# GFNet mixing and SoLU block: the step back in even and odd halves on quarters of the array, and the second product in another PSUM bank

## The chip, the cores and the metric

The kernel runs on one core of a Trainium2 chip. The metric is the device time in microseconds (us). Six names of engines are used: PE is TensorE's matmul stream, PEld its weight loads (they overlap the matmuls), DVE is VectorE, ACT ScalarE, POOL GpSimd, and SP the engine that only issues DMAs. Each engine takes its own instructions in order; across engines they are held together by semaphores.

## What is computed

The first half filters eight sequences of 3136 tokens with 256 channels by a multiplication in frequency space; the second is a feed-forward block over all 25088 tokens with the SoLU activation and a layer norm.

```python
X = np.fft.rfft(x, axis=1)                      # x: (8, 3136, 256)
y = np.fft.irfft(X * (filt_r + 1j * filt_i), n=3136, axis=1)
h = y.reshape(25088, 256) @ w_in                # w_in: (256, 1024)
e = np.exp(h - h.max(-1)); sm = e / (e.sum(-1) + 1e-9)
solu = h * sm
ln = (solu - solu.mean(-1)) / np.sqrt(solu.var(-1) + 1e-6) * g_ln
out = ln @ w_out                                # w_out: (1024, 256)
```

All of it is in float32.

## The kernel before

**The transform.** 3136 = 49 x 64. An example is transformed in three steps: a first one over the 49 residues (`first` or `first_quarters`), the spectrum (`forward`, `multiply`, `inverse`, seven units an example), and the step back over 49 (`fetch_back`, then `back`). Between the steps the rows lie in DRAM (`d1`, `d2`). The step back of an example has 8 pieces of 4 columns. A piece reads 100 rows (25 frequencies of four kinds) with all 256 channels. For each half of the channels (`cb`), `back` makes one matmul for each of the 4 columns: the rows are the stationary operand (100 x 128), and the table `wi_t` (100 x 98) streams. The 98 results are 49 tokens of column n and 49 tokens of the mirrored column 63 - n; the table holds both signs. ACT copies the 128 x 392 result into `y`, the SBUF buffer that holds two examples, channels on partitions.

**The block.** Tokens are taken 128 at a time; one such tile is a step k, and there are 196 steps and 9 more to empty the pipeline. Two steps, an even one k = 2j and the odd one behind it, make a pair j. For a pair, both products (with w_in and with w_out) are made by Strassen's scheme with seven multiplications each: `product(j, m)` and `project(p, m)`, m = 1 to 7. They are issued in the order 1, 5, 2, 6, 3, 4, 7 (even step: products 1, 2, 6, 7 and projections 5, 3, 4; odd step: products 5, 3, 4 and projections 1, 2, 6, 7). `keep` and `keep_out` copy an unfinished sum out of its PSUM bank on ACT, `finish` and `finish_out` take the last one on DVE and add what was kept. A bank goes on accumulating after it was read: products 1, 6, 5, 3 share bank 0, product 2 has bank 1, products 7 and 4 share bank 2; projections have two banks. So a later product must wait until the reader of the sum before has read its bank. Of one tile DVE makes: `finish` (L701 or L704) with the running minimum, `normalize` (L723, L725, L728), `turn` (L738, a transpose in blocks of 32). ACT makes the exponential (L712) and the square sum (L730). SP regroups the turned rows by DMA, POOL forms the sums that Strassen's scheme needs (L658).

**The order.** It is written out by hand in `step(k)`. The transform of examples 1 to 7 is spread over the steps by PLAN; its parts are put into lists by step: `stores` (ahead of the step's first product), `products` (in the middle), `early` (behind it, ahead of the next products), `late` and `loads` (at the end). In an even step with a step back, `back` of the first half of the channels stands in `early` and that of the second half in `late`; `forward` stands in `early` too, `multiply(i, 0)` in `late`, and `multiply(i, 1)`, `inverse`, `difference` and `first_quarters` in the odd step behind. Example 1 has its step back at steps 16 to 22, odd ones too.

**PSUM.** Eight banks: two of tag `t` (products 2, the step back, the first transform), two for a unit of the spectrum, two in `ps_m` (banks 0 and 2 of the products), two for the projections.

**Lines.** L353 step-back matmul, L356 its copy; L680 products, L792 projections; L690 `keep`, L804 `keep_out`; L701 and L704 `finish`; L809 `finish_out` with nothing kept, L811 with a kept part; L313 to L315 `multiply`; L245 `difference`; L260 `first_quarters` and L265 its copies; L292 `forward` (`pb`) and `inverse` (`pc`).

Of the kernel before, what the change touches and what calls it, by code (L numbers as in the profile page):

```python
# [9 lines left out]
FP32 = mybir.dt.float32  # L10
I32 = mybir.dt.int32
AFT = mybir.ActivationFunctionType
ALU = mybir.AluOpType
# [4 lines left out]
P = 128  # L18
B, S, C = 8, 3136, 256
# [30 lines left out]
def dft_tables():  # L50

    n1, s, q, m = np.arange(N1), np.arange(NS), np.arange(NQ), np.arange(NH)
    ph = 2 * np.pi * (np.outer(n1, s) % N1) / N1
    w = np.cos(ph), -np.sin(ph)
    v = 2 * np.cos(ph), -2 * np.sin(ph)
    v[0][:, 0], v[1][:, 0] = 1.0, 0.0
    wf = np.zeros((2, N1, NS, 4))
    wi = np.zeros((NS, 4, 2, N1))

    for a, part, sign in ((0, 0, 1), (1, 1, -1), (2, 1, 1), (3, 0, 1)):  # L70
        other = -1 if a == 3 else 1
        wf[0, :, :, a], wf[1, :, :, a] = sign * w[part], other * w[part]
        wi[:, a, 0], wi[:, a, 1] = sign * v[part].T / S, other * v[part].T / S

    kap = np.where(q[:, None] < 32, s + N1 * q[:, None], s + N1 * (95 - q[:, None]))
    sg = np.where(q < 32, 1.0, -1.0)
    th = 2 * np.pi * (((N2 - 1 - 2 * m)[:, None, None] * kap) % (2 * S)) / (2 * S)
    d = np.zeros((2, 2, NH, 2 * NP, NQ))
    d[0, :, :, :NS] = np.stack([np.cos(th), np.sin(th)]).transpose(0, 1, 3, 2)
    d[1] = d[0] * sg  # L80
    d = d.reshape(2, 2 * NH, NP, 2, NQ)
    there = d.transpose(2, 0, 1, 3, 4).reshape(NP, P, 2 * NQ)
    back = d.transpose(2, 3, 4, 0, 1).reshape(NP, P, 2 * NQ)
    de = np.stack([there, back], 2).reshape(NP, P, 2, 2, NQ)
    f32 = np.float32
    wq = np.zeros((2, 64, 2, 64))
    wq[:, :N1, :, :NK // 2] = wf[1].reshape(N1, NS, 2, 2).transpose(0, 3, 1, 2).reshape(N1, 2, NK // 2)
    return wf.reshape(NR, NK).astype(f32), wq.reshape(P, 2, 64).astype(f32), \
        wi.reshape(NK, NR).astype(f32), de.astype(f32)


@with_exitstack
def kernel(
# [8 lines left out]
    out: bass.AP,  # L102
):
    nc = tc.nc
    wf_host, wq_host, wi_host, de_host = dft_tables()
    wf_dram = nc.inline_tensor(wf_host, name="wf_tbl").ap()
    wq_dram = nc.inline_tensor(wq_host, name="wq_tbl").ap()
    wi_dram = nc.inline_tensor(wi_host, name="wi_tbl").ap()
    de_dram = nc.inline_tensor(de_host, name="de_tbl").ap()

    def pool(name, bufs, space=None, stack=ctx):
# [6 lines left out]
    small = pool("sm", 4)  # L118

    d1 = [dram.tile([NS, P, C], FP32, name=f"d1_{e}") for e in range(B)]  # L120
    d2 = [dram.tile([NS, P, C], FP32, name=f"d2_{e}") for e in range(B)]
    f_dram = dram.tile([NP, 2, NQ, 2, C], FP32, name="f_dram")

    wf_t = consts.tile([NR, NK], FP32, name="wf_t")
    wq_t = consts.tile([P, 2, 64], FP32, name="wq_t")
    wi_t = consts.tile([NK, NR], FP32, name="wi_t")


    w_in_sb = consts.tile([P, 7, DFF // 2], FP32, name="w_in_sb")
# [205 lines left out]

    t4s = {}

    def fetch_back(e, ch, rows_pool, split=None):

        split = split or whole  # L340
        if rows_pool is not None:
            t4s[e, ch] = rows_pool.tile([P, NCH, C], FP32, name=f"t4_{e}_{ch}", tag="r")[0:NK]
        split(
            (nc.sync.dma_start if split is by_16 else nc.gpsimd.dma_start, nc.sync.dma_start), t4s[e, ch],
            d2[e].rearrange("s (a n) c -> (s a) n c", a=4)[:, NCH * ch:NCH * ch + NCH, :])

    def back(e, ch, cb, evac):

        ps = ps_t.tile([P, 512], FP32, name=f"py_{e}_{ch}_{cb}", tag="t")

        psv = ps[:, 0:NCH * NR].rearrange("p (m r) -> p m r", r=N1)
        for i in range(NCH):
            nc.tensor.matmul(out=psv[:, i:2 * NCH - i:2 * NCH - 1 - 2 * i, :],  # L353
                             lhsT=t4s[e, ch][:, i, cb * P:cb * P + P], rhs=wi_t, start=True, stop=True)
        t0, last = e % 2 * S, N2 // NCH - 1
        evac(out=y[:, cb, t0:t0 + S].rearrange("p (r m j) -> p m j r", m=N2 // NCH, j=NCH)[  # L356
            :, ch:last + 1 - ch:last - 2 * ch], in_=psv.rearrange("p (m j) r -> p m j r", m=2))


    with ExitStack() as st:  # L360
# [163 lines left out]
        for i in range(units):  # L524
            if i + 2 < units:
                start(i + 2)
            sp.multiply(i, 0, nc.vector.tensor_tensor)
            sp.multiply(i, 1, nc.gpsimd.tensor_tensor)
            pss = [ps_t.tile([P, 2, C], FP32, name=f"pc_0_{i}_{u}", tag="t") for u in range(2)]
            idle(pss[0])  # L530
            sp.inverse(i, pss)
            sp.store(i, nc.scalar.dma_start)
            if i == 0:
                nc.gpsimd.dma_start(out=wi_t, in_=wi_dram)
                nc.gpsimd.dma_start(out=wq_t, in_=wq_dram)
                nc.gpsimd.dma_start(out=g_sb, in_=moe_g_ln.rearrange("(k p) -> p k", p=P))
            elif i != 2:
                begin({1: 2, 3: 3, 4: 4, 5: 5, 6: 6}[i])
# [2 lines left out]
        for ch in range(pieces):  # L541
            t4s[0, ch] = rows_t4[0:NK, NCH * ch:NCH * ch + NCH]
        for ch in range(pieces):
            fetch_back(0, ch, None, by_16)
        fetch_second()
        for i0, n, rows in ((0, 4, P), (4, 4, P), (8, NP - 9, P), (NP - 1, 1, NQ)):
            f, at = filters[i0]
# [19 lines left out]
    def psum(name):  # L567
        return ps_t.tile([P, 2, C], FP32, name=name, tag="t")
# [102 lines left out]
    def product(j, m):  # L671

        bank = {1: 0, 6: 0, 5: 0, 3: 0, 2: 1, 7: 2, 4: 2}[m]
        if m in (1, 2, 7):
            ms[j, bank] = (ps_t.tile([P, DFF // 2], FP32, name=f"m{m}_{j}", tag="t") if m == 2 else
                           ps_m.tile([P, DFF // 2], FP32, name=f"m{m}_{j}", tag=f"m{bank}"))
        lhs = {1: tokens(2 * j, 0), 2: tokens(2 * j, 1), 4: tokens(2 * j + 1, 1)}
        lhsT = lhs[m] if m in lhs else sums[j][{5: 0, 6: 1, 7: 2, 3: 3}[m]]
        w = {1: 0, 2: 1, 3: 2, 5: 3, 6: 4, 7: 5, 4: 6}[m]
        nc.tensor.matmul(out=ms[j, bank], lhsT=lhsT, rhs=w_in_sb[:, w, :],  # L680
                         start=m in (1, 2, 7), stop=True, skip_group_check=True)
# [115 lines left out]
    def out_half(p, i, n):  # L797
        if p not in ots:
            ots[p] = wk2.tile([P, 2, C], FP32, name=f"ot_{p}", tag="ot")
        return ots[p][:, i, P * n:P * n + P], rss[p // 2][:, 2 * (p % 2) + i:2 * (p % 2) + i + 1]  # L800
# [4 lines left out]

    def finish_out(p, i, n, kept, bank):
        ot, rs = out_half(p, i, n)
        if kept is None:
            nc.vector.tensor_scalar(out=ot, in0=pos[p, bank], scalar1=rs, scalar2=None, op0=ALU.mult)  # L809
        else:  # L810
            nc.vector.scalar_tensor_tensor(out=ot, in0=pos[p, bank], scalar=rs,  # L811
                                           in1=out_half(p, *kept)[0], op0=ALU.mult, op1=ALU.add)

    def store_out(p):
        g, second = divmod(p, 2)
# [18 lines left out]
    for e in range(1, B):  # L834
# [41 lines left out]
        assert S * (e - 1) <= P * (back_at[0] // 2 * 2) and P * (back_at[-1] + 2) <= S * e // P // 2 * 2 * P  # L876
        for ch, t in enumerate(back_at):
            row_loads.append((
                t, t - 1, spectrum_at[-1] + 2, lambda e=e, ch=ch: fetch_back(e, ch, pools["r"])))
            for cb in range(KD):  # L880
                (early, late)[cb][t].append(
                    lambda e=e, ch=ch, cb=cb: back(e, ch, cb, nc.scalar.copy))
    row_loads.sort(key=lambda load: load[0])
    for n, (t, latest, earliest, load) in enumerate(row_loads):

# [10 lines left out]
    def step(k):  # L896
# [39 lines left out]
        if not odd:  # L936
            if hid:
                product(j, 6)
                keep(j, k + 1, 0)
            if proj:  # L940
                project(p, 3)
                project(p, 4)
            if 0 <= j - 3 < pairs:
                regroup(j - 3, 1)
            if 0 <= j - 4 < pairs:
                project_sums(j - 4, 1)
            if hid:
                product(j, 7)
        else:
            if proj:  # L950
                project(p, 1)
                keep_out(p, 0, (0, 0))
                project(p, 2)
                finish_out(p, 0, 0, (0, 0), 1)
            if hid:
                product(j, 3)
                product(j, 4)
            if 0 <= j - 3 < pairs:
                project_sums(j - 3, 0)
                if (j - 3) % 2 == 0:  # L960
                    regroup_deviations((j - 3) // 2)
            if proj:
                project(p, 6)
                project(p, 7)
        if 2 <= k < blocks + 2:
            normalize(k - 2)
        if not odd:
            if proj:
                finish_out(p, 0, 1, None, 0)
                finish_out(p, 1, 0, (1, 0), 1)  # L970
                store_out(p)
        else:
            if hid:
                finish(j, k - 1, 1, None, 0)
                finish(j, k, 0, (k, 0), 2)
            if proj:
                keep_out(p, 1, (1, 0))
# [39 lines left out]
```

## Time and profile before

| | us |
|---|---|
| three runs | 1677.1, 1690.1, 1691.35 |
| median | 1690.1 |
| span of the profiled execution | 1680.2 |
| mean granted TensorE clock | 0.988 of full speed |

The trace was read by pairs of steps, from the start of one product 1 to that of the next:

| what the pair holds beside the block | us |
|---|---|
| nothing (from step 168 on) | 12.26 to 12.95 |
| step back alone (150 to 164) | 14.05 to 14.18 |
| step back and spectrum (132 to 138) | 16.50 to 16.77 |
| step back, spectrum, first transform (40) | 17.78 |
| two pieces of example 1 and a spectrum (16 to 22) | 17.52 to 20.22 |

A line of the groups reads: line, engine, operation, output<-input, shapes, count | busy us, mean ns of one | idle time of the engine just before them and what ended it. In float32 every matmul of the program is two in the trace. [...]their spacing, not their duration, is what one costs.

### The profile page before, as it was taken

The page shows a single profiled execution, that of the slowest core. Times are in us where ns is not written, and L with a number is a line of the kernel's source. Part 1 is how long each engine was busy: PE and PEld are TensorE (multiplying, and loading weights), DVE is VectorE, ACT ScalarE, POOL GpSimd, SP SyncE. Part 2 cuts the span into 40 slices and gives each one's busy share as a digit, 9 for nine tenths or more (in the row PEclk, how much of TensorE's full clock was granted, in tenths as well). Part 3 has the DMA queues.
Part 4 walks back from the last instruction along what each step waited for, and adds up shares of the span by engine and source line. Part 5 has one row for each costly group of instructions (what it writes and reads, how often), then busy time and mean ns, then how long its engine had stood idle before and what let it go on. Part 6 is the DMA issues. An engine that isn't in the chain of part 4 may idle for free.

```text
span 1680.2 us, 31072 instructions
## 1 busy us (share of the span) xinstructions
PE 1597.7 (95%) x10022; PEld 1094.7 (65%) x10022; DVE 1260.4 (75%) x2619; ACT 939.3 (56%) x1730; POOL 1120.8 (67%) x1268
## 2 busy tenths in 40 slices
PE   5798899999999999999999999999999999999996
PEld 1353356766766676667766676667776777777776
DVE  1676887788777877886878777887778767787773
ACT  2154455656655565566655656556565566655551
POOL 4444786577676766697577866687576766676674
PEclk8999999999999999999999999999999999999999
DMA  9886868786787668865786667766775444444443
GB/s 264 254 278 202 255 180 243 196 220 182 191 224 222 178 182 236 228 182 150 210 243 195 176 166 220 229 181 161 204 213 161 117 125 123 103 106 105 109 112 95
DMA packets 375957, 311.72 MB, mean 186 GB/s; under 512 B 61514, under 2 KB 341571, under 8 KB 375795
## 3 DMA queue, kind: packets, MB, share of 16 engines
q1 hardware_dynamic: 306260, 169.81, 38.5%
q0 software_dynamic: 32640, 101.65, 20.5%
q10 hardware_dynamic: 36896, 38.28, 8.2%
q8 instruction: 81, 1.33, 0.3%
q14 instruction: 80, 0.66, 0.1%
HBM read 124.83 MB, written 81.50 MB: 123 GB/s over the span
## 4 chain that ended last, share of the span: by engine, by line
PE 64%; DMA 17%; DVE 8%; POOL 3%; issue 3%; SPq 2%; ACT 1%; ACTq 0%; DVEq 0%; POOLq 0%
PE m L680 26%; PE o L792 25%; DMA solu_t<-turn 7%; PE py L353 5%; DMA x<-in_x_dram 2%; DMA t<-d 2%; PE pa L260 2%; PE pb L292 2%; PE pc L292 2%; SPq L750 2%; DVE h L728 2%; DVE turn L738 1%; DMA out_dram<-ot 1%; PE pa L217 1%; DVE diff L245 1%
## 5 line engine op out<-in xcount | busy, mean ns | idle before, releaser
L730 ACT ACTIVATE e<-h,nmu 128x1024 f32<-128x1024 f32 x196 | 225.3, 1149 | 360.3 <-DVE h L728 358.8
L792 PEld LDWEIGHTS o<-w_out_sb,solu_t 128*128 128x128 f32 x3136 | 380.3, 192 | 57.8 <-issue 40.7
L792 PE MATMUL o<-w_out_sb,solu_t 128*128 128x128 f32 x3136 | 400.5, 276 | 9.1 <-DVE rsum L723 6.3
L680 PE MATMUL m<-w_in_sb,s 128*128 128x512 f32 x784 | 401.8, 604 | 4.6 <-ACT h L690 2.5
L792 PEld LDWEIGHTS o<-w_out_sb,u 128*128 128x128 f32 x2352 | 305.2, 191 | 147.4 <-issue 113.8
L658 POOL TENSOR_TENSOR u<-solu_t 128x512 f32<-128x512 f32 x98 | 145.3, 1483 | 311.0 <-DMA solu_t<-turn 179.0
L680 PE MATMUL m<-w_in_sb,y 128*128 128x512 f32 x588 | 313.8, 617 | 15.9 <-DVE nmax L704 12.8
L792 PE MATMUL o<-w_out_sb,u 128*128 128x128 f32 x2352 | 312.3, 276 | 7.0 <-ACT ot L804 6.3
L728 DVE SCALAR_TENSOR_TENSOR h<-e,rsum,h 128x1024 f32<-128x1024 f32 x196 | 289.1, 1475 | 6.9
L811 DVE SCALAR_TENSOR_TENSOR ot<-o,rs_t,ot 128x128 f32<-128x128 f32 x294 | 102.5, 349 | 206.6 <-ACT ot L804 170.3
L690 ACT COPY h<-m 128x512 f32<-128x512 f32 x294 | 173.5, 590 | 130.8 <-PE m L680 116.2
L738 DVE STREAM_TRANSPOSE turn<-h 128x1024 f32<-128x1024 f32 x196 | 242.3, 1236 | 0.8
L712 ACT ACTIVATE e<-h,nmax 128x1024 f32<-128x1024 f32 x196 | 226.1, 1154 | 0.0
L658 POOL TENSOR_TENSOR u<-solu_t,u 128x512 f32<-128x512 f32 x98 | 142.7, 1456 | 87.2 <-PE o L792 83.3
L704 DVE CUSTOM_DVE_ANT_0 h<-m,h 128x512 f32<-128x512 f32 x196 | 133.2, 679 | 82.2 <-ACT h L690 59.3
L680 PEld LDWEIGHTS m<-w_in_sb,y 128*128 128x128 f32 x588 | 95.1, 192 | 124.5 <-DVE nmax L704 67.9
L356 ACT COPY y<-py 128x392 f32<-128x392 f32 x128 | 109.6, 856 | 105.4 <-PE py L353 103.8
L353 PEld LDWEIGHTS py<-wi_t,t 100*128 100x128 f32 x1024 | 132.3, 192 | 53.9 <-issue 40.4
L680 PEld LDWEIGHTS m<-w_in_sb,s 128*128 128x128 f32 x784 | 124.0, 191 | 65.9 <-issue 45.7
L658 POOL TENSOR_TENSOR solu_t<-solu_t,solu_t 128x512 f32<-128x512 f32 x98 | 150.8, 1538 | 7.7
L658 POOL TENSOR_TENSOR u<-u,solu_t 128x512 f32<-128x512 f32 x98 | 136.9, 1397 | 0.7
L353 PE MATMUL py<-wi_t,t 100*128 100x98 f32 x1024 | 131.6, 273 | 0.7 <-DMA t<-d 0.4
(108 smaller groups left out, 1978.3 us busy)
## 6 DMA issues: line engine op xcount, KB each, us to landing
solu_t<-turn SPq DMA_DIRECT2D x784, 128.0 KB
out_dram<-ot SPq DMA_DIRECT2D x196, 128.0 KB
t<-d POOLq DMA_DIRECT2D x56, 400.0 KB, 4.9
d<-x POOLq DMA_DIRECT2D x100, 200.0 KB, 5.3
f<-f_dram POOLq DMA_DIRECT2D x39, 512.0 KB, 6.9
d<-g POOLq DMA_DIRECT2D x39, 512.0 KB, 5.1
t<-d ACTq DMA_DIRECT2D x36, 512.0 KB
x<-in_x_dram SPq DMA_DIRECT2D x112, 98.0 KB
```

The source lines that it names most:

```text
L353: nc.tensor.matmul(out=psv[:, i:2 * NCH - i:2 * NCH - 1 - 2 * i, :], lhsT=t4s[e, ch][:, i, cb * P:cb * P + P], rhs=wi_t, start=True, stop= ...
L356: evac(out=y[:, cb, t0:t0 + S].rearrange("p (r m j) -> p m j r", m=N2 // NCH, j=NCH)[:, ch:last + 1 - ch:last - 2 * ch], in_=psv.rearrange ...
L658: nc.gpsimd.tensor_tensor(out=out, in0=in0, in1=in1, op=op)
L680: nc.tensor.matmul(out=ms[j, bank], lhsT=lhsT, rhs=w_in_sb[:, w, :], start=m in (1, 2, 7), stop=True, skip_group_check=True)
L690: nc.scalar.copy(out=h_half(k, i), in_=ms[j, 0])
L704: nc.vector.tensor_tensor_reduce(out=h_half(k, i), in0=ms[j, bank], in1=h_half(*kept), scale=1.0, scalar=sofar, op0=ALU.add, op1=ALU.min, ...
L712: nc.scalar.activation(out=e, in_=hs[k], func=AFT.Exp, bias=nmaxs.pop(k)[:, 1:2], scale=-1.0, accum_out=esum)
L728: nc.vector.scalar_tensor_tensor(out=solu, in0=e, scalar=rsum, in1=solu, op0=ALU.mult, op1=ALU.mult, accum_out=nmu)
L730: nc.scalar.activation(out=e, in_=solu, func=AFT.Square, bias=nmu, scale=-float(DFF), accum_out=variances[g][:, i:i + 1])
L738: nc.vector.transpose(out=turns[g][:, :, i, :], in_=solus.pop(k).rearrange("p (f j) -> p f j", j=32))
L792: nc.tensor.matmul(out=pos[p, bank], lhsT=lhs[:, f, :], rhs=w[:, f, :], start=f == 0 and m in (1, 2, 7), stop=True, skip_group_check=True)
L811: nc.vector.scalar_tensor_tensor(out=ot, in0=pos[p, bank], scalar=rs, in1=out_half(p, *kept)[0], op0=ALU.mult, op1=ALU.add)
```

## The change

The table `wi` has, for a column and its mirror, the same numbers up to the sign: two of the four kinds of rows enter with the same sign, two with opposite ones. So the product with 98 columns is replaced by two with 49, over 50 rows each. In SBUF, `fetch_back` now puts the even rows on partitions 0 to 49 and the odd rows on 64 to 113, in one DMA of 128 rows (the rows above 50 in either half belong to the next example in DRAM and are not used; for this all `d2` lie in one tensor, in reversed order). `back_halves` makes for each half of the channels, each column, each half of the rows and each 64 channels one matmul (50 rows x 64 channels stationary, the table `wb_t` of 49 columns streaming): 32 for a piece, on the four 64 x 64 quarters of the array, even rows into one bank of tag `t`, odd rows into the other. ACT copies the even half into SBUF, over the rows that were read. `join_halves` then forms, on DVE, even + odd for the columns and even - odd for the mirrored ones, and writes them into `y`. Example 0 keeps the old way.

`back_halves` stands in `early` as a whole (the sixth piece of example 1, which has the same step as the fifth, in `late`), `join_halves` in `late`. Since the step back holds both banks of tag `t` until its join, product 2 leaves that tag for the bank of products 7 and 4. The scaling of the projection that DVE did after `normalize` (`finish_out(p, 0, 1, None, 0)`) becomes a `keep_out` on ACT between projections 3 and 4.

```diff
+    wb = np.zeros((2, 64, N1))
+    wb[:, :NK // 2] = wi[:, :, 0].reshape(NS, 2, 2, N1).transpose(2, 0, 1, 3).reshape(2, NK // 2, N1)
...
-    d2 = [dram.tile([NS, P, C], FP32, name=f"d2_{e}") for e in range(B)]
+    d2_all = dram.tile([B * NS, P, C], FP32, name="d2")
+    d2 = [d2_all[(B - 1 - e) * NS:(B - e) * NS] for e in range(B)]
...
+    def fetch_back(e, ch):
+
+        t4s[e, ch] = t4 = pools["r"].tile([P, NCH, C], FP32, name=f"t4_{e}_{ch}", tag="r")
+        s0 = (B - 1 - e) * NS
+        rows = d2_all[s0:s0 + P // 4].rearrange("s (b j n) c -> j (s b) n c", b=2, j=2)
+        nc.gpsimd.dma_start(out=t4, in_=rows[:, :, NCH * ch:NCH * ch + NCH, :])
+
+    joins = {}
+
+    def back_halves(e, ch, pss):
+
+        t4 = t4s.pop((e, ch))
+        views = [ps.rearrange("p a c -> p (a c)")[:, 0:KD * NCH * N1].rearrange(
+            "p (c i r) -> p c i r", c=KD, i=NCH) for ps in pss]
+        for cb in range(KD):
+            for i in range(NCH):
+                for g in range(2):
+                    rows = slice(64 * g, 64 * g + NK // 2)
+                    for h in range(2):
+                        c0 = cb * P + 64 * h
+                        nc.tensor.matmul(out=views[g][64 * h:64 * h + 64, cb, i, :],
+                                         lhsT=t4[rows, i, c0:c0 + 64], rhs=wb_t[rows],
+                                         start=True, stop=True)
+        even = t4.rearrange("p i c -> p (i c)")[:, 0:KD * NCH * N1]
+        nc.scalar.copy(out=even, in_=pss[0].rearrange("p a c -> p (a c)")[:, 0:KD * NCH * N1])
+        joins[e, ch] = even.rearrange("p (c i r) -> p c i r", c=KD, i=NCH), views[1]
+
+    def join_halves(e, ch):
+
+        even, odd = (v.rearrange("p c i r -> p c r i") for v in joins.pop((e, ch)))
+        t0, last = e % 2 * S, N2 // NCH - 1
+        to = y[:, :, t0:t0 + S].rearrange("p c (r m j) -> p m c r j", m=N2 // NCH, j=NCH)
+        nc.vector.tensor_tensor(out=to[:, ch], in0=even, in1=odd, op=ALU.add)
+        nc.vector.tensor_tensor(out=to[:, last - ch], in0=even[:, :, :, ::-1], in1=odd[:, :, :, ::-1],
+                                op=ALU.subtract)
...
-            ms[j, bank] = (ps_t.tile([P, DFF // 2], FP32, name=f"m{m}_{j}", tag="t") if m == 2 else
-                           ps_m.tile([P, DFF // 2], FP32, name=f"m{m}_{j}", tag=f"m{bank}"))
+            ms[j, bank] = ps_m.tile([P, DFF // 2], FP32, name=f"m{m}_{j}", tag=f"m{min(bank, 1)}")
...
-            for cb in range(KD):
-                (early, late)[cb][t].append(
-                    lambda e=e, ch=ch, cb=cb: back(e, ch, cb, nc.scalar.copy))
+            (late if ch and t == back_at[ch - 1] else early)[t].append(lambda e=e, ch=ch: back_halves(
+                e, ch, [psum(f"py_{e}_{ch}_{g}") for g in range(2)]))
+            late[t].append(lambda e=e, ch=ch: join_halves(e, ch))
...
                 project(p, 3)
+                keep_out(p, 0, (0, 1))
                 project(p, 4)
...
-                finish_out(p, 0, 1, None, 0)
                 finish_out(p, 1, 0, (1, 0), 1)
```

More of the change, by code (lines that the diff above doesn't have):

```diff
@@ L87, in dft_tables @@
     wq[:, :N1, :, :NK // 2] = wf[1].reshape(N1, NS, 2, 2).transpose(0, 3, 1, 2).reshape(N1, 2, NK // 2)
+    wb = np.zeros((2, 64, N1))
+    wb[:, :NK // 2] = wi[:, :, 0].reshape(NS, 2, 2, N1).transpose(2, 0, 1, 3).reshape(2, NK // 2, N1)
     return wf.reshape(NR, NK).astype(f32), wq.reshape(P, 2, 64).astype(f32), \
-        wi.reshape(NK, NR).astype(f32), de.astype(f32)
+        wi.reshape(NK, NR).astype(f32), wb.reshape(P, N1).astype(f32), de.astype(f32)
 @with_exitstack
@@ L104 @@
     nc = tc.nc
-    wf_host, wq_host, wi_host, de_host = dft_tables()
+    wf_host, wq_host, wi_host, wb_host, de_host = dft_tables()
     wf_dram = nc.inline_tensor(wf_host, name="wf_tbl").ap()
@@ L108 @@
     wi_dram = nc.inline_tensor(wi_host, name="wi_tbl").ap()
+    wb_dram = nc.inline_tensor(wb_host, name="wb_tbl").ap()
     de_dram = nc.inline_tensor(de_host, name="de_tbl").ap()
@@ L126 @@
     wi_t = consts.tile([NK, NR], FP32, name="wi_t")
+    wb_t = consts.tile([P, N1], FP32, name="wb_t")
     w_in_sb = consts.tile([P, 7, DFF // 2], FP32, name="w_in_sb")
@@ L336, with fetch_first_back @@
     t4s = {}
[L338 to L345, printed above, removed]
+    def fetch_first_back(ch):
+        by_16((nc.sync.dma_start, nc.sync.dma_start), t4s[0, ch],
+              d2[0].rearrange("s (a n) c -> (s a) n c", a=4)[:, NCH * ch:NCH * ch + NCH, :])
@@ L535 @@
                 nc.gpsimd.dma_start(out=wq_t, in_=wq_dram)
+                nc.gpsimd.dma_start(out=wb_t, in_=wb_dram)
                 nc.gpsimd.dma_start(out=g_sb, in_=moe_g_ln.rearrange("(k p) -> p k", p=P))
@@ L543 @@
         for ch in range(pieces):
-            fetch_back(0, ch, None, by_16)
+            fetch_first_back(ch)
         fetch_second()
@@ L807, in finish_out @@
         ot, rs = out_half(p, i, n)
[L808 to L812, printed above, removed]
+        nc.vector.scalar_tensor_tensor(out=ot, in0=pos[p, bank], scalar=rs,
+                                       in1=out_half(p, *kept)[0], op0=ALU.mult, op1=ALU.add)
     def store_out(p):
@@ L878 @@
             row_loads.append((
-                t, t - 1, spectrum_at[-1] + 2, lambda e=e, ch=ch: fetch_back(e, ch, pools["r"])))
-            for cb in range(KD):
-                (early, late)[cb][t].append(
-                    lambda e=e, ch=ch, cb=cb: back(e, ch, cb, nc.scalar.copy))
+                t, t - 1, spectrum_at[-1] + 2, lambda e=e, ch=ch: fetch_back(e, ch)))
+            (late if ch and t == back_at[ch - 1] else early)[t].append(lambda e=e, ch=ch: back_halves(
+                e, ch, [psum(f"py_{e}_{ch}_{g}") for g in range(2)]))
+            late[t].append(lambda e=e, ch=ch: join_halves(e, ch))
     row_loads.sort(key=lambda load: load[0])
```

## The prediction

> **What bounds the kernel now.** I read the busy shares first, then TensorE's waits, then the timelines of TensorE (PE) and VectorE (DVE) over single pairs of steps. The page's first part says that PE is nearly always at work:
>
> ```profile
> PE 1597.7 (95%) x10022; PEld 1094.7 (65%) x10022; DVE 1260.4 (75%) x2619; ACT 939.3 (56%) x1730; POOL 1120.8 (67%) x1268
> L353 PE MATMUL py<-wi_t,t 100*128 100x98 f32 x1024 | 131.6, 273 | 0.7 <-DMA t<-d 0.4
> L356 ACT COPY y<-py 128x392 f32<-128x392 f32 x128 | 109.6, 856 | 105.4 <-PE py L353 103.8
> ```
>
> The second and third line are the step back today. A share of 75% would make DVE look harmless. The timelines of one pair with a step back, a forward/inverse unit and a first transform in it (the pair of 17.8 us from 499.2) say otherwise. Columns: start, duration, instruction, idle time before it.
>
> ```profile
> 506.90 0.35 DVE L811 SCALAR_TENSOR_TENSOR ot<-o,rs_t,ot 128x128 f32<-128x128 f32 x1 [0.55 <-PE o L792]
> 507.17 0.68 DVE L313 TENSOR_TENSOR pr<-pb,f 128x512 f32<-128x512 f32 x1
> ...
> 511.12 0.64 DVE L704 CUSTOM_DVE_ANT_0 h<-m,h 128x512 f32<-128x512 f32 x1
> ...
> 513.63 0.34 DVE L811 SCALAR_TENSOR_TENSOR ot<-o,rs_t,ot 128x128 f32<-128x128 f32 x1
> ```
> ```profile
> 505.81 1.06 PE L792 MATMUL o<-w_out_sb,solu_t 128*128 128x128 f32 x8
> ...
> 511.96 1.02 PE L680 MATMUL m<-w_in_sb,y 128*128 128x512 f32 x2
> ...
> 514.03 1.16 PE L792 MATMUL o<-w_out_sb,solu_t 128*128 128x128 f32 x8 [0.15 <-DVE rsum L723]
> ```
>
> DVE waits at 506.90 for PE's projection 4 (505.81, ends 506.86), and then works without a gap up to L811 at 513.97. PE's projection 7 (514.03) overwrites the bank that this L811 reads, and so it waits, for 0.15 us. That is a ring: 7.17 us of DVE from projection 4's end to projection 7, then PE's work round to the next projection 4 (10.62 us). Product 4 (511.96) likewise starts just after L704 (ends 511.77) has read its bank. In pairs without a first transform the ring closes at the next product 1, behind L701; there, too, it sits at balance:
>
> ```profile
> 1283.80 1.13 PE L680 MATMUL m<-w_in_sb,y 128*128 128x512 f32 x2 [0.26 <-DVE h L701]
> ```
>
> So in the pairs with a spectrum, PE and DVE are both full between those two points, though DVE has 1.5 us idle elsewhere in the pair.
>
> [...] step-back matmuls of 98 columns with 128 weight columns start 112 ns apart[...], no faster than those of 128 columns. [...] the first 64x64 load at 502.908 comes 0.203 us after the last full matmul's start, 0.09 more than the usual 0.112; leaving costs about another 0.19 (0.09 idle, and 0.10 of weight load in the open). [...] the ACT copy L356, which writes single words 64 apart, took 856 ns for 392 where L690 needs 586 for 512 contiguous.
>
> **Part by part.** Pairs are counted from PLAN, for examples 2 to 7: A, step back with spectrum and first transform, 15 pairs (mostly 17.8 to 18.4 us each); B, step back with spectrum alone, 12 (16.5 to 17.1); C, with first transform alone, 4 (15.3); D, alone, 17 (14.05 to 14.3). Example 1 has 8 pieces in 4 pairs (17.5 to 20.2).
>
> *PE.* Removed per piece: two visits of 8 matmuls at 112 ns, 1.79 us. Added: 32 matmuls in two passes, 64, over four tiles. Four at once: [...] the 64x64 pairs in the trace start 13.3 ns apart, so 53 ns a set. 16 sets: 0.93 us. Where the piece stands beside `forward` (31 of 56) the mode changes are paid already: 0.86 us saved; else 0.58 (25). Were PE alone the bound: 31 x 0.86 + 25 x 0.58 = 41 us. Bounds: perfect overlap 0.85 us[...].
>
> *DVE.* Added per piece: two joins of 392 elements, one source in SBUF and one in PSUM, both stepping 49 words, writing runs of four. L313 (512 elements, PSUM and SBUF) starts its successor 0.60 us later[...]. [...] I take 1.5 us for both, 0.95 to 2.1. They stand right behind L811 and ahead of `multiply`, `difference`, `turn` and L704: inside the ring. The ACT copy that they wait for is done by then (its input is ready 4 us earlier). Removed: L809, 348 ns; it sits ahead of a 0.55 us wait for projection 4, so it is worth nothing.
>
> *ACT.* Two copies of 856 ns become one contiguous one of about 0.5; a 363 ns `keep_out` is added behind projection 3. It delays the Square L730, which is not in the ring. Gain or loss about nothing while ACT idles 44% of the time; bounds -0.2 to +0.3 us per pair.
>
> *Banks, queues, DMA.* Product 2 now waits for L704's read of product 4's bank. That L704 follows L701, for which product 1 waits, by 0.75 us, and product 1 and projection 5 take 1.75 us on PE: covered. Product 7's bank is read by L704 3.6 us before product 7 comes: covered. The step back needs both banks of the `t` tag; the ACT copies of `pa` leave them at 519.09, the step back starts at 519.73: covered by 0.6 us. Rows read back grow from 100 to 128 (400 to 512 KB, 6 MB of 312), POOL issues as many DMAs as before; PE waited 0.4 us for these in all, and one landed some 10 us early: nothing, at worst 1 us per example. Their slot is freed by DVE rather than PE, some 4 us later, against a lead of two steps.
>
> *Sum per pair.* A: ring 7.17 + 1.5, and PE's side + 0.07 (0.93 for 0.86 between projection 7 and 4): +1.57. B: DVE from projection 4 to L701's end is 8.71 with 0.14 of idle, so 8.57 + 1.5 = 10.07; PE's way from product 1 to projection 4's end 7.63 + 0.07; in all 17.8 against a mean of 16.7: +1.1. D: DVE's rows from L811 to L701 sum to 5.3, with the joins 6.8, against PE's 7.74 - 0.86 = 6.88 (projection 4's end 1398.14 to product 1 at 1405.88): still PE's, -0.55. C: the `diff` of 0.95 more, 7.75 against 8.0 on PE: -0.5. Example 1: about 10.1 + 7.7 = 17.8 in four pairs, 71 against 75 now, but its step 20 sends two pieces through the same banks at once, so PE waits for a join there, about 3 us; together nothing, -4 to +5. Total: 15 x 1.57 + 12 x 1.1 - 4 x 0.5 - 17 x 0.55 = 23.6 + 13.2 - 2.0 - 9.4 = **+25 us**. With joins of 0.95: +8; with 2.1: +58. The profiled execution spans 1680.2 us, inside the range of the runs (1677.1 to 1691.35), so I add to the median: 1690 + 25 = **1715**.
>
> **Rivals.** (a) *PE decides, faster*: 41 us less, 1649. It needs the joins to be hidden: two of them within about 0.54 us, where gains and losses above cancel, or a ring slacker than the two lines with 0.15 and 0.26 show. PE's 95% speaks for it, DVE's gapless stretch against it. (b) *Joins at full rate*: +8, 1698, no change to be seen. [...] (c) *Small matmuls don't overlap* in their tiles: 1.85 us for 0.93, 56 x 0.92 = +52 more, 1768. Against it: the 64x64 matmuls in the trace do run four abreast, with loads below the streams[...]. That the change doesn't do what it says I exclude: the changed code issues the 50-row matmuls, both joins and the moved copy at the places named, and nothing else is moved.
>
> **Numbers.** About 1%, 17 us, is what a measurement can tell. Forecast 0.58, (a) 0.10, (b) 0.17, (c) 0.15. Forecast and (c) are slower, 0.73; (b) same, 0.17; (a) faster, 0.10. The range 1692 to 1760 takes in (b), the dear joins and part of (c); it leaves out (a) and the rest of (c).
>
> **What would show it.** Joins of 0.75 to 0.85 us each right behind L811 in DVE's timeline; new PE waits at product 4, projection 7 or product 1 for DVE, some 1 to 2 us per A and B pair; A pairs near 19.4 us, D pairs near 13.6; the step back about 1 us per piece on PE. I am wrong if joins take under 0.5 us, if A pairs get shorter, or if the step back itself takes over 1.5 us.

## The result, and the profile after

| | kernel before | kernel after |
|---|---|---|
| median of four runs, us | 1689.4 | 2118.7 |
| lowest and highest, us | 1677.1, 1691.35 | 2114.4, 2124.4 |
| span of the profiled execution, us | 1680.2 | 2116.0 |
| mean granted TensorE clock | 0.988 | 0.899 |

The ratio is 1.257 (interval 1.252 to 1.262): 429 us slower, where the prediction had 25 and a range that ended at 1760.

The page of the kernel after, its busy shares, the step back's matmuls (L367) and, from its last part, the row of the read-back (count, KB each, median us from issue to landing); then, from the groups by line, the ACT copy (L371) and one of the joins (L379):

```profile
PE 1706.4 (81%) x12710; PEld 1138.6 (54%) x12710; DVE 1295.9 (61%) x2633; ACT 905.7 (43%) x1772; POOL 1106.6 (52%) x1269
...
L367 PE MATMUL py<-wb_t,t 50*64 50x49 f32 x3584 | 97.8, 273 | 235.1 <-DMA t<-d 182.4
...
t<-d POOLq DMA_DIRECT2D x56, 512.0 KB, 18.7
```
```profile
L379 DVE TENSOR_TENSOR y<-t,py 128x392 f32<-128x392 f32 x56 | 45.8, 818 | 1.8 <-ACT t L371 1.8
...
L371 ACT COPY t<-py 128x392 f32<-128x392 f32 x56 | 27.3, 488 | 174.5 <-PE py L367 174.5
```

No engine is the bound any more: PE falls from 95 to 81%, DVE from 75 to 61%. The joins are there, at 0.82 us, and ACT's copies have gone from 856 to 488 ns. What is new stands behind the bars: PE was idle for 235.1 us ahead of the step back's matmuls, where it had been 0.7, and the rows read back land 18.7 us after their issue. The lower clock comes with it: 0.899 here, 0.978 again in the kernel of experiment 1 that has the same matmuls and reads the rows faster. In the kernel before the same row reads:

```profile
t<-d POOLq DMA_DIRECT2D x56, 400.0 KB, 4.9
```

A quarter more bytes, and nearly four times as long. The list of waits of the kernel after (engine, tile and line, what it waited for, us in total, times, longest) shows whom it hurts:

```profile
POOL u L695 <- DMA solu_t<-turn: 565.4, 73, 18.2
...
DVE ot L844 <- PE o L828: 335.3, 94, 15.3
DVE ot L844 <- ACT ot L840: 321.3, 140, 10.6
...
PE py L367 <- DMA t<-d: 182.4, 36, 16.3
```

The largest is not the step back's own wait. POOL waits 565.4 us for regrouped rows, another transfer, which the change did not touch. In the kernel before that was:

```profile
POOL u L658 <- DMA solu_t<-turn: 179.0, 47, 7.9
```

One pair with nothing but a step back shows the ring. Timelines of POOL and PE in the kernel after (start, duration, instruction, idle time before it):

```profile
1734.18 1.27 POOL L695 TENSOR_TENSOR u<-solu_t 128x512 f32<-128x512 f32 x1 [11.69 <-DMA solu_t<-turn]
...
1736.74 0.85 POOL L352 DMA_DIRECT2D t<-d  x1
...
1753.36 1.27 POOL L695 TENSOR_TENSOR u<-solu_t 128x512 f32<-128x512 f32 x1 [10.00 <-DMA rs_t<-rows]
...
1755.91 0.88 POOL L352 DMA_DIRECT2D t<-d  x1
```
```profile
1747.79 1.02 PE L716 MATMUL m<-w_in_sb,y 128*128 128x512 f32 x2
1752.11 1.96 PE L367 MATMUL py<-wb_t,t 50*64 50x49 f32 x64 [3.29 <-DMA t<-d]
```

POOL issues the load at 1736.74, its rows land some 15 us later, PE starts the step back at 1752.11, and POOL's first sum for the next pair comes at 1753.36, 19.2 us after the one shown first (here the last rows to land were the small `rs_t`, which SP loads as it does the regrouped ones). Behind it stands the next load. A pair of type D (step back alone) now takes 20.2 us, against 14.15.

The trace also has the packets of a DMA. These are the 4096-byte ones of that load, start in us:

```
1738.378 1738.388 | 1738.858 1738.868 | 1739.338 1739.348 | 1739.811 1739.820 | 1739.966 1739.976 | ...
... | 1751.092 1751.103 | 1751.271 ...          (128 packets in 12.9 us)
```

They come two at a time, 64 pairs at 0.20 us.

### The profile page after: what moved, and what is told of

It is laid out like the page before. It is cut to its first block, busy times and chain, and to the rows that moved or that the text cites. A ratio compares the mean times of both kernels' runs of the same rounds, so it can differ in the third digit from the quotient of the medians.

```text
span 2116.0 us, 36712 instructions
## 1 busy us (share of the span) xinstructions
PE 1706.4 (81%) x12710; PEld 1138.6 (54%) x12710; DVE 1295.9 (61%) x2633; ACT 905.7 (43%) x1772; POOL 1106.6 (52%) x1269
## 3 DMA queue, kind: packets, MB, share of 16 engines
q0 software_dynamic: 83744, 108.29, 18.7%
## 4 chain that ended last, share of the span: by engine, by line
DMA 50%; PE 32%; issue 4%; DVE 4%; POOL 4%; SPq 3%; ACT 1%; POOLq 0%; ACTq 0%; DVEq 0%
DMA solu_t<-turn 19%; DMA t<-d 16%; PE o L828 13%; PE m L716 12%; DMA d<-g 5%; SPq L786 3%; DMA d<-x 2%; DMA x<-in_x_dram 2%; PE pb L297 2%; PE py L367 2%; DMA de<-de_tbl 2%; DMA out_dram<-ot 1%; POOL solu_t L695 1%; POOL u L695 1%; DMA rs_t<-rows 1%
## 5 line engine op out<-in xcount | busy, mean ns | idle before, releaser
L695 POOL TENSOR_TENSOR u<-solu_t 128x512 f32<-128x512 f32 x98 | 137.2, 1400 | 790.9 <-DMA solu_t<-turn 565.4
L716 PE MATMUL m<-w_in_sb,s 128*128 128x512 f32 x784 | 425.1, 646 | 31.0 <-ACT h L726 29.3
L828 PEld LDWEIGHTS o<-w_out_sb,u 128*128 128x128 f32 x2352 | 335.1, 207 | 173.5 <-issue 126.6
L828 PEld LDWEIGHTS o<-w_out_sb,solu_t 128*128 128x128 f32 x3136 | 393.5, 197 | 56.7 <-issue 37.5
L828 PE MATMUL o<-w_out_sb,u 128*128 128x128 f32 x2352 | 339.1, 291 | 12.8 <-ACT ot L840 9.1
L367 PE MATMUL py<-wb_t,t 50*64 50x49 f32 x3584 | 97.8, 273 | 235.1 <-DMA t<-d 182.4
L764 DVE SCALAR_TENSOR_TENSOR h<-e,rsum,h 128x1024 f32<-128x1024 f32 x196 | 275.5, 1405 | 6.9
L367 PEld LDWEIGHTS py<-wb_t,t 50*64 50x64 f32 x3584 | 88.4, 187 | 282.2 <-issue 149.9
L840 ACT ACTIVATE ot<-o,rs_t 128x128 f32<-128x128 f32 x392 | 142.6, 364 | 92.6 <-PE o L828 79.1
L695 POOL TENSOR_TENSOR solu_t<-solu_t,solu_t 128x512 f32<-128x512 f32 x98 | 137.2, 1400 | 7.7
L335 ACT COPY g<-pc 128x512 f32<-128x512 f32 (+1 forms) x98 | 51.0, 569 | 194.2 <-DMA d<-g 134.5
## 6 DMA issues: line engine op xcount, KB each, us to landing
t<-d POOLq DMA_DIRECT2D x56, 512.0 KB, 18.7
```

Of the source, the lines that this page charges most:

```text
L367: nc.tensor.matmul(out=views[g][64 * h:64 * h + 64, cb, i, :], lhsT=t4[rows, i, c0:c0 + 64], rhs=wb_t[rows], start=True, stop=True)
L695: nc.gpsimd.tensor_tensor(out=out, in0=in0, in1=in1, op=op)
L764: nc.vector.scalar_tensor_tensor(out=solu, in0=e, scalar=rsum, in1=solu, op0=ALU.mult, op1=ALU.mult, accum_out=nmu)
L828: nc.tensor.matmul(out=pos[p, bank], lhsT=lhs[:, f, :], rhs=w[:, f, :], start=f == 0 and m in (1, 2, 7), stop=True, skip_group_check=True)
L840: nc.scalar.activation(out=out_half(p, *to)[0], in_=pos[p, 0], func=AFT.Copy, scale=rs)
```

## The experiments

**1. One load or two.** First theory: the packets come two at a time because the outermost dimension of the DMA has the size 2. Two loads of 64 rows each read the same bytes into the same places. The reverse goes with it: the kernel before, its 100 rows read in the order even, odd by one DMA of that form.

```diff
-        nc.gpsimd.dma_start(out=t4, in_=rows[:, :, NCH * ch:NCH * ch + NCH, :])
+        for j in range(2):
+            nc.gpsimd.dma_start(out=t4[64 * j:64 * j + 64], in_=rows[j, :, NCH * ch:NCH * ch + NCH, :])
```
```diff
+            nc.gpsimd.dma_start(out=t4s[e, ch], in_=d2[e].rearrange("s (b j n) c -> j (s b) n c", b=2, j=2)[
+                :, :, NCH * ch:NCH * ch + NCH, :])
```

> The changed kernel, but each piece's rows are read back by two DMAs of 64 rows (even rows, odd rows) instead of one whose source has the two halves as its outermost dimension. Theory 1 ([...]64 rows of 4 KB each at 0.18 us, 12 to 13 us on the engines and 15 to 19 us to landing, and holds up both the step back and the regroup DMAs[...]): landing falls to 4 to 7 us, PE's wait of 182 us for these rows goes to under 5 us, POOL's wait for the regrouped rows from 565 back to some 180 to 250 us, and the time to 1690 to 1740 us. Theory 2 (the 430 us come from the step back itself: its waits for banks and the joins in VectorE's ring): still over 1950 us.

> The kernel before, with one thing changed: the 100 rows of a piece are read back in the order even 50, odd 50, in one DMA whose source has these two halves as its outermost dimension; the table for the matmul has its rows in the same order. Matmuls, copies and joins are those of before. Theory 1: [...]50 x 0.18 = 9 us on the engines and 11 to 15 us to landing, and the kernel is slower than before by 100 to 350 us with nothing else changed. Theory 2: within 1% of before.

Two loads: 1732.7 us, ratio 1.026 (1.023 to 1.030). The kernel before with rows in that order: 1973.2 us, 1.169 (1.164 to 1.174); a second table was needed for it, which moves later tiles by 416 bytes. No run has that move alone; the moves of experiment 5 cost 2.9% at most, so they do not explain 16.9. The read-back rows of the two kernels, two loads first:

```profile
t<-d POOLq DMA_DIRECT2D x112, 256.0 KB, 4.9
```
```profile
t<-d POOLq DMA_DIRECT2D x56, 400.0 KB, 14.9
```

And POOL's wait for regrouped rows in both, in the same order:

```profile
POOL u L696 <- DMA solu_t<-turn: 249.4, 72, 8.9
```
```profile
POOL u L665 <- DMA solu_t<-turn: 426.3, 67, 14.5
```

With two loads sixteen packets start within 0.22 us (1395.042 to 1395.265), and 386 of the 429 us are gone. So the form of the one DMA was the cause, not its bytes. The runs have an outermost dimension of 2 with 128 rows (18.7 us to landing) and with 100 (14.9), and loads whose outermost dimension is the 64 rows (4.9); what other sizes would do was not shown. Why the regrouped rows get late with such a load was not shown either. Shown is that the lateness comes with this load and goes with it: POOL waits 565.4 us for them with the one load, 249.4 with two, 179.0 in the kernel before.

**2. What is left: 2.6%, and the joins' place.** With two loads the prediction's own rows can be read. DVE, then PE, in one pair of type A (step back, spectrum, first transform) of that kernel:

```profile
527.05 0.35 DVE L845 SCALAR_TENSOR_TENSOR ot<-o,rs_t,ot 128x128 f32<-128x128 f32 x1 [2.28 <-PE o L829]
527.32 0.82 DVE L380 TENSOR_TENSOR y<-t,py 128x392 f32<-128x392 f32 x1
528.06 0.81 DVE L381 TENSOR_TENSOR y<-t,py 128x392 f32<-128x392 f32 x1
528.79 0.68 DVE L318 TENSOR_TENSOR pr<-pb,f 128x512 f32<-128x512 f32 x1
...
532.92 0.65 DVE L741 CUSTOM_DVE_ANT_0 h<-m,h 128x512 f32<-128x512 f32 x1
```
```profile
522.10 1.15 PE L368 MATMUL py<-wb_t,t 50*64 50x49 f32 x64
523.07 1.11 PE L297 MATMUL pb<-t,de 64*64 64x256 f32 x16
```

The two joins hold DVE for 0.74 and 0.73 us from start to next start, right behind the `finish_out` (L845), and a step back PE for 0.97. To see what the joins cost where they stand, one kernel puts them ahead of that `finish_out`, in front of the wait for projection 4 (2.28 us here), and one, whose diff is not printed, leaves out the joins of examples 2 to 7, and with them a part of the work.

```diff
-            late[t].append(lambda e=e, ch=ch: join_halves(e, ch))
+            (late if ch and t == back_at[ch - 1] or t % 2 else ahead_of_out)[t].append(
+                lambda e=e, ch=ch: join_halves(e, ch))
...
             normalize(k - 2)
+        for job in ahead_of_out[k]:
+            job()
```

> As two_loads, but in even steps the join stands on VectorE ahead of the last finish_out of the step (where VectorE waits about 1.5 us for projection 4) instead of behind it. Theory A (the prediction's ring: two joins of 0.75 us between projection 4 and projection 7 or product 1 lengthen every pair with a spectrum): 27 pairs x 1.5 = 40 us less than two_loads, 30 to 50. Theory B (the joins are hidden in two_loads already): within 8 us of two_loads.

> As two_loads, but the joins of examples 2 to 7 are left out: y keeps the values of examples 0 and 1, so the outputs of examples 2 to 7 are not those of the reference. It shows what the cheaper step back is worth when VectorE gets no work for it. Theory A (in pairs with a spectrum and a first transform PE's saving of 0.86 us lies inside VectorE's ring and brings nothing; only pairs without, 17 x 0.55, and some of the B pairs gain): 1675 to 1705 us, A pairs not under 17.7 us. Theory B (PE is the bound, the prediction's rival a): 41 us less than before but for the start, 1645 to 1660, A pairs near 17.0.

Early joins: 1712.0 us, 1.013 (1.009 to 1.017). No joins: 1714.0, 1.016 (1.012 to 1.020). So where they stood the joins cost some 20 us; early they cost nothing that these two runs tell apart. But even without them 1.6% was left, and pairs of type A stayed at 19.4 us (18.45 before).

**3. The parts that were costed at nothing.** The kernel before with product 2 in the bank of products 7 and 4, and with `keep_out` in the place of the `finish_out` with nothing kept.

```diff
+            ms[j, bank] = ps_m.tile([P, DFF // 2], FP32, name=f"m{m}_{j}", tag=f"m{min(bank, 1)}")
...
+                keep_out(p, 0, (0, 1))
...
-                finish_out(p, 0, 1, None, 0)
```

> The kernel before with two parts of the change alone: product 2 in the bank of products 7 and 4, and the scaling of a projection by keep_out on ACT instead of finish_out on VectorE; the step back is that of before. The prediction held both for covered: within 8 us of before. Rival: sharing the bank makes product 2 or product 7 wait for VectorE in most pairs, 98 x 0.3 us or more: at least 25 us slower.

1685.3 us, 1.0007 (0.9988 to 1.0025). Both are free, as predicted.

**4. Two misses.** In pairs of type A with early joins, `difference` ran beside POOL's sum; the theory was that these two held each other up. They were put behind the `finish_out` of the odd step; a second kernel, with the same move, issued one of the two loads from ACT instead of POOL.

```diff
-                stores[t].append(lambda sp=sp, i=i: sp.difference(i))
-                products[t].append(lambda sp=sp, i=i: sp.sum(i))
+                (ahead_of_three if t % 2 else stores)[t].append(lambda sp=sp, i=i: sp.difference(i))
+                (ahead_of_three if t % 2 else products)[t].append(lambda sp=sp, i=i: sp.sum(i))
```

> As two_loads_join_early, but in odd steps the difference of the first transform on VectorE, and POOL's sum behind it, stand behind the finish_out that projection 7 waits for, instead of at the step's start. In two_loads_join_early that difference took 1.77 us in an A pair (0.95 before), inside the ring. Theory A (A pairs, 19.3 us there, are bound by VectorE's way from projection 4 to projection 7): 15 pairs x 1 to 1.8 us = 15 to 27 us less than two_loads_join_early, A pairs near 17.5. Rival (the A pairs are late for another reason: rows of x, regrouped rows): within 6 us.

> As diff_late, but the second of the two loads of a piece (the odd rows) is issued by ACT instead of POOL. If POOL's queue, which got 56 more DMAs of some 0.55 us each, makes the sums late: 5 to 15 us less than diff_late. If POOL has room: within 5 us; slower by 5 us or more if ACT, in order, has to wait at that load for the rows to be stored.

1715.5 us, 1.018 (1.013 to 1.024), and 1719.0, 1.017 (1.012 to 1.023). No gain: pairs of type A went from 19.31 to 19.25 us, although PE's wait for DVE at product 4 fell from 34.3 us in all to 4.6. The loss lay elsewhere.

**5. Where a tile lies.** One number differed where both kernels do the same work: in the tail, the 512-byte packets of the regrouped rows took 32.0 ns each in the kernel before and 44.4 after. The change adds a constant, `wb_t`, of 196 bytes, for which 224 are set aside; every tile behind it lies 224 bytes further in SBUF. First the kernel before got only a shift, and three of the kernels above had `wb_t` padded to 256 bytes.

```diff
-    wi_t = consts.tile([NK, NR], FP32, name="wi_t")
+    wi_t = consts.tile([NK, NR + 8], FP32, name="wi_t")[:, 0:NR]
```
```diff
-    wb_t = consts.tile([P, N1], FP32, name="wb_t")
+    wb_t = consts.tile([P, 64], FP32, name="wb_t")[:, 0:N1]
```

> The kernel before with nothing changed but a tile of constants made 32 bytes longer, so that every later tile in SBUF (y, the regrouped rows, the rows read back) begins 32 bytes further and on no multiple of 64 bytes. In the kernel before the 512-byte packets of the regrouped rows take 32.0 ns each in the tail, in the kernel after and in the one with two loads 44.4 ns, where both do the same work. Theory: the new constant wb_t moved every later tile by 224 bytes, and this is what makes the packets longer; here they take some 44 ns, with regrouped rows and x landing later, and the time is 1700 to 1715 us. Rival: the place in SBUF has no effect and the longer packets come from what the change does; the packets take 32 ns and the time is 1689 within 5 us.

> The kernel after with two loads of 64 rows each, and wb_t made 64 columns wide (49 used), so that later tiles begin on multiples of 64 bytes again. Theory of the shifted tiles: the packets of the regrouped rows fall from 44.4 to 32 ns, pairs of type A from 20.0 to 19.2 us or less, example 1 back to near 18.7 us, the time to 1708 to 1722 us from 1732.7. Rival without effect: 1733 within 6 us and 44 ns packets.

> As the run with two loads and the join ahead of the last finish_out, with wb_t 64 columns wide. Theory of the shifted tiles: from 1712 to 1685 to 1700 us, about level with the kernel before: pairs of type D keep their 0.55 us gain, pairs of types A and B come close to the kernel before. Rival: 1712 within 6 us, what pairs of type A still lose (19.3 against 18.45 us) being the difference taken beside POOL's sum and not the packets.

> The kernel after with its one load for each piece[...], and wb_t 64 columns wide. [...]its packets get shorter if the theory of the shifted tiles holds: 2090 to 2118 us against 2118.7, landing of the rows near 18 us still. If the shift were the main cause of the 429 us, it would fall near 1733 us; if it has no part in it, 2118 within 8 us.

A shift of 32 bytes, with nothing else changed, makes the kernel before 2.4% slower (1726.8 us, 1.019 to 1.029). Padding takes it away wherever it is put:

| | `wb_t` as it is | `wb_t` padded |
|---|---|---|
| one load (kernel after) | 2118.7, 1.257 | 2051.2, 1.216 (1.211 to 1.222) |
| two loads | 1732.7, 1.026 | 1709.2, 1.013 (1.010 to 1.017) |
| two loads, joins early | 1712.0, 1.013 | **1672.2, 0.9915** (0.9888 to 0.9941) |

The last one is faster than both kernels, than the one before by 0.85% (0.6 to 1.1). Of it, PE's share on the page and PE's wait for DVE at product 4 (L717, behind the `finish` at L741) in the list of waits; then the same wait with two loads, `wb_t` padded too, and the joins where the change put them:

```profile
PE 1572.2 (94%) x12710; PEld 1052.6 (63%) x12710; DVE 1313.1 (78%) x2633; ACT 904.7 (54%) x1772; POOL 1142.0 (68%) x1325
```
```profile
PE m L717 <- DVE nmax L741: 23.9, 28, 2.5
```
```profile
PE m L717 <- DVE nmax L741: 56.8, 41, 2.5
```

PE is back at 94%. The theory took multiples of 64 bytes for the rule. Seven more shifts of the kernel before tested that, and which tiles matter. Five lengthen the same constant, or the tile of `y`; two put unused bytes between the tiles, ahead of or behind the pool of `turn` and the outputs (`wk2`):

```diff
     wk2 = pool("wk2", 2)
+    pool("pad", 1).tile([P, 8], FP32, name="pad")
```

> The kernel before with the tile of constants made 64 bytes longer instead of 32. Theory that only the place against multiples of 64 bytes counts: packets of the regrouped rows 32 ns and 1686 us within 6. Rival that any shift of y and the tiles behind it costs (another order of addresses, other neighbours): slower by 1 to 3%, as with 32 bytes (1726.8).

> The kernel before with y, the weights and the constants where they were, and only the tiles behind y (rows of x, regrouped rows, rows read back, outputs, scalars) 32 bytes further. Theory that DMA writes into those tiles pay for it: packets longer than 32 ns and slower by 1.5 to 3%, as with everything shifted (1726.8). Rival that TensorE, ScalarE or VectorE pay on y or the weights: 1686 us within 6.

> The kernel before with y and every tile behind the constants 128 bytes further. Shifts of 32 and 64 bytes made the packets of the regrouped rows 36.3 and 36.5 ns (31.9 before) and the time 2.4 and 1.9% longer; a shift of 256 bytes (wb_t made 64 columns wide) left them at 33. Theory that blocks of 256 or 512 bytes count: some 36 ns again and 1.5 to 3% slower. Rival that multiples of 128 bytes are enough: 32 ns and 1686 us within 6.

> The kernel before with all tiles behind the constants 224 bytes further, exactly the shift that wb_t brings. Theory that the place alone makes the packets 43 to 44 ns in the kernel after: 42 to 45 ns here too, and 2 to 4% slower. Rival that the place gives 36 ns, as with 32 and 64 bytes, and the rest comes from other work of the change: 36 ns and 2% slower.

> The kernel before with all tiles behind the constants 256 bytes further, the shift that wb_t with 64 columns brings. Shifts of 32, 64, 128 and 224 bytes all made the 512-byte packets longer (36 to 43 ns) and the time 1.2 to 2.6% longer. Theory that only the place within blocks of 256 bytes counts: 32 ns and 1686 us within 8. Rival that any shift off the old places costs: packets over 34 ns and 1% slower or more.

> The kernel before with y, the outputs and the block turn, out of which regrouped rows are copied, where they were, and only the tiles behind them (the regrouped rows solu_t, rows of x, rows read back) 32 bytes further. Theory that writes by the DMA pay: packets some 36 ns and 1.5 to 3% slower. Rival that reads out of turn pay: 32 ns and 1686 us within 8.

> The reverse: turn and the outputs 32 bytes further, the tiles behind them 256 bytes further (so at a multiple of 256 as before). Theory that writes pay: 32 ns and 1686 us within 8. Rival that reads pay: some 36 ns and 1.5 to 3% slower. Were both to pay, each of these two runs would show a part, near 34 ns.

| tiles moved in the kernel before | by bytes | 512-byte packets, mean ns | the same without the transform | ratio of times |
|---|---|---|---|---|
| none | 0 | 31.9 | 32.0 | 1 |
| all behind the constants | 32 | 36.3 | 34.7 | 1.024 (1.019 to 1.029) |
| the same | 64 | 36.5 | 35.7 | 1.019 (1.016 to 1.023) |
| the same | 128 | 36.1 | 35.9 | 1.012 (1.008 to 1.015) |
| the same | 224 | 42.8 | 44.5 | 1.026 (1.022 to 1.030) |
| the same | 256 | 31.8 | 32.0 | 0.9999 (0.998 to 1.002) |
| only those behind `y` | 32 | 36.6 | 34.8 | 1.029 (1.022 to 1.035) |
| all behind `turn` and the outputs (regrouped rows, rows of x, filters, rows read back, and tiles of the engines) | 32 | 34.4 | 32.0 | 1.017 (1.012 to 1.021) |
| the block `turn` (source of the regrouped rows) and the outputs | 32 | 34.4 | 35.0 | 1.004 (1.002 to 1.005) |

"Without the transform" is the stretch from 190 to 20 us before the end. The rule of 64 bytes is wrong (64 and 128 cost too); 256 are free. Moving only what lies behind `y` costs as much as moving everything, so `y` and the weights have no part in it that shows.

The equal means of the last two rows hide two different things. Without the transform, moving `turn` and the outputs makes the packets longer (35.0, as moving all by 32 bytes does with 34.7), and moving what lies behind them does not (32.0): there the place of the source decides. While the transform runs, the move of what lies behind `turn` makes other transfers slower too: the 1024-byte packets of ACT's queue take 67.9 ns against 60.5 in the kernel before (57.6 with the source moved), and the filters `f` land 8.6 us after their issue instead of 6.9 (7.2). So most of the time is lost with the tiles behind `turn`, and not with the source of the regrouped rows. Which of these tiles cost it stays open, as no run moves one of them alone.

The share of the DMA engines that the queue of the regrouped rows took (queue, packets, MB, share), with shifts of 224 and of 256 bytes:

```profile
q1 hardware_dynamic: 306260, 169.81, 46.0%
```
```profile
q1 hardware_dynamic: 306260, 169.81, 38.5%
```

The same packets and bytes, and a share larger by a fifth. With two loads and `wb_t` as it is the queue has 46.3%, with it padded 38.7%: the shift alone accounts for it.

## Why the prediction was wrong

Pairs of types A (step back, spectrum, first transform), B (step back, spectrum), C (step back, first transform), D (step back alone), mean us:

| pairs | before | predicted | after | two loads | two loads, padded | joins early, padded |
|---|---|---|---|---|---|---|
| A, 15 | 18.45 | 20.02 | 27.84 | 20.02 | 19.56 | 18.63 |
| B, 12 | 16.70 | 17.80 | 26.45 | 18.04 | 17.85 | 16.57 |
| C, 4 | 15.25 | 14.75 | 20.73 | 15.22 | 14.93 | 14.74 |
| D, 17 | 14.15 | 13.60 | 20.21 | 13.57 | 13.59 | 13.62 |
| example 1, 4 | 18.72 | 18.7 | 28.03 | 20.33 | 19.50 | 19.33 |

**The step that failed** is the one on the rows read back: "Rows read back grow from 100 to 128 (400 to 512 KB, 6 MB of 312), POOL issues as many DMAs as before; PE waited 0.4 us for these in all, and one landed some 10 us early: nothing, at worst 1 us per example." It weighed bytes, issues and a wait of 0.4 us, and not how many packets of the new form would be under way at a time. The access pattern stood in the diff, with `j` of size 2 outermost. In its place the runs showed packets two at a time, a landing of 18.7 us instead of 4.9, and a cost of 342 us (2051.2 less 1709.2, `wb_t` padded in both) or 386 us (2118.7 less 1732.7).

**A term is missing** from the sum: the place of the tiles. The table `wb_t` was never costed. Alone in the kernel before its shift is worth 2.6%, some 43 us; padding it saved 23.5 us with two loads, 40 with early joins and 67 in the kernel after. So it is no fixed sum; that each kernel has other slack for late transfers would explain it, and is not shown.

**The rest of the sum held in the main.** With both taken away, the change (with 56 issues more on POOL than were costed) runs at 1.0133 of the kernel before, which on 1690 is 1712 us; the prediction was 1715. By types, padded: A +1.11 us (predicted +1.57), B +1.15 (+1.1), C -0.32 (-0.5), D -0.56 (-0.55), example 1 +0.78 (0). That the total agrees so closely is in part luck: the 15 pairs of A lose 7 us less than foretold, example 1 loses 3 more, and the 32 other pairs ahead of step 168 lose 4 that were not costed (15.61 to 15.74 us each). That A with `wb_t` unpadded is +1.57 to the digit is chance too: the shift is part of it, and costs these pairs 0.95 us in the kernel before (19.40).

- Joins: 1.5 us for both were the author's estimate, which no trace of the kernel before shows; measured were 0.72 to 0.75 each nearly throughout (two loads, padded). Rival (b), joins at full rate, falls: L313, whose 512 elements take 0.60 us to the next start in the kernel before (507.17 to 507.77), scaled to 392 gives 0.46 each.
- Step back on PE: predicted 0.93 us a piece, measured 0.97 beside `forward`, 1.08 ahead of a product. Rival (c), 1.85 us, falls. Both figures were the author's estimates (starts alone, sixteen sets of 53 ns, give 0.85): the trace before has matmuls on quarters with 256 columns, whose sets of four start 0.216 us apart (503.176 to 503.392), and none with 49.
- The ring: PE's wait for DVE at product 4 went from 12.8 us before to 56.8 with two loads, padded. Of these, 29.4 lie in the 15 pairs of A and 14.7 in the 12 of B, 2.0 and 1.2 us a pair, where 1 to 2 were foretold. With the joins ahead of the wait for projection 4 it is 23.9. So the mechanism was right, but not its place: the ring closes at product 4, in B too, where the prediction had product 1.
- Rival (a), PE decides: right for pairs of type D in every kernel with two loads. Even with the joins moved and the tiles back in place it is not right for A (+0.18) and B (-0.13), where it has -0.86. Its 41 us aren't reached: 1672.2 is 11 us less than the median of the kernel before in the same series.
- Banks and `keep_out` at nothing: right (1.0007).
- Slips in the working, which don't decide: by its own terms joins of 0.95 us give about +10, not +8. Type D is set against PE's 7.74 less 0.86, though the saving without `forward` was put at 0.58. The 1.85 us of rival (c) aren't worked out from any trace.

## What to carry to other kernels

Read the access pattern of every changed DMA for its outermost dimension before weighing its bytes: a factor of 2 put there for a layout made the rows land after 18.7 us instead of 4.9 here, and another transfer paid more than the one that was changed (waits of 565.4 us for regrouped rows, 182.4 for the rows read back); splitting it into one DMA for each value took one more issue (112 of 0.55 us on POOL with two loads, 56 of 0.86 with one). A new constant moves all tiles that are allocated behind it: pad constants so that the buffers behind them, which DMAs read and write in small packets, keep their place within 256 bytes (a shift by 224 cost 2.6% here, one by 256 nothing, 0.9999), and compare packet times in a stage where both kernels do the same work. And work on a full engine costs by its place in the order: the same joins were 21 us cheaper (37 with `wb_t` padded) ahead of a wait than behind it.

## What the runs showed of the hardware

- One load of 128 rows of 4 KB with an outermost dimension of 2, two packets at a time: 0.20 us a pair, 12.9 us in all, 18.7 us from issue to landing; the same bytes in two loads of 64 rows land after 4.9 us.
- 512-byte packets inside SBUF take 31.9 ns with all tiles where the kernel before has them, 31.8 when all are shifted by 256 bytes, 36 by 32, 64 or 128 and 42.8 by 224. Of these five shifts only that by 256 costs nothing. Once the transform is over, the source's place counts (35.0 ns with `turn` and the outputs shifted by 32, 32.0 with the targets). Why shifts of 32, 64 and 128 bytes give nearly the same packets was not shown.
- The 32 matmuls of a piece, 64 in the trace, of 50 rows x 64 channels and 49 columns, over the four quarters, take 0.97 us from start to the next operation's start where that is a matmul on quarters too, 1.08 where it is a product on the whole array.
- An elementwise operation of 392 elements on DVE, with sources that step 49 words, one in SBUF and one in PSUM, holds DVE for 0.72 to 0.75 us from start to next start (two loads, padded; 0.74 and 0.73 in the timeline of experiment 2).
